# Merging the score and value visits of a banded attention kernel, with zero products in TensorE's planned gaps

## The chip, the cores and the metric

The kernel runs on one core of one Trainium2 chip. The metric is the time of one execution on the device in microseconds. The kernel before takes 534.74 us, the median of three runs (534.62 to 535.40).

## The reference

Eight batches, eight heads, 576 positions, 64 channels a head; then a gated MLP over the 4608 tokens, from 512 to 1024 and back to 512 channels. The weights arrive as 64-bit floats.

```python
# attention, B, H, S, D = 8, 8, 576, 64; stride = 32
scores = scale * np.matmul(q, k.transpose(0, 1, 3, 2))
mask_local = (rel >= 0) & (rel < stride)                       # heads 0 to 3
mask_strided = (rel >= 0) & (pos[None] % stride == pos[:, None] % stride)  # heads 4 to 7
scores = np.where(masks, scores, -1000000000.0)
scores = scores - np.max(scores, axis=-1, keepdims=True)
attn = np.exp(scores)
attn = attn / (np.sum(attn, axis=-1, keepdims=True) + 1e-09)
x = (attn @ v).transpose(0, 2, 1, 3).reshape(B, S, H * D)
# gated MLP: w_in 512 x 1024, conv_w 3 x 1024, w_out 1024 x 512
h = np.maximum(x @ w_in, 0.0)
conv_out[:, s] = sum(conv_w[k] * h[:, s + k - 1] for k in range(3))
gate = 1.0 / (1.0 + np.exp(-conv_out))
return (h * gate @ w_out).astype(np.float32)
```

## The kernel before

**Attention** works on items: item n is a pair of heads of one batch, and there are 32 (four to a batch). Both masks are banded in blocks of 32 rows once the positions of the strided heads are reordered, so an item's scores are ten blocks of 64 columns on 128 partitions, 128 x 640. TensorE writes the mask as a product (L449) and adds the scores (L458). VectorE takes the maximum (L470) and subtracts it (L471), ScalarE takes the exponent (L473), VectorE sums (L474) and inverts (L476). Then the result is divided and turned in one of two ways, chosen by `TURN`: GpSimd multiplies (L492) and VectorE transposes (L494), or VectorE makes a diagonal of the inverses (L478), TensorE multiplies by it (L486) and ScalarE copies the result (L490). The values product (L514) gives 128 x 576. It leaves PSUM as two parts, a high one by a ScalarE cast (`xh`, L549) and a low one by a VectorE subtraction (`xl`, L574). For the first four items `LOW` chooses another way for the low part: TensorE subtracts the high part in PSUM (L569) and ScalarE copies the rest (L572).

**The MLP** runs over nine groups g of 512 tokens. The first layer (L607) has eight column blocks f, each the sum over four channel blocks, the second (L667) four output blocks over eight f. Each product is made of three matmuls of 128x512, high by high, low by high, high by low; such a triple is the unit of TensorE's order. Between the layers a column block takes relu (L624), a scaling by the middle tap (L634 or L637), two multiply-adds (L643), a sigmoid (L646), the gate (L648) and a split into high and low parts (L431, L434). Ahead of all that, the weights are converted from 64-bit words (L334 to L343, eight times 128 x 1024) and split, partly with products by the unit matrix on TensorE (`wA`, L411 to L413; `wQ`, L418 and L419).

**PSUM.** A tile `psR` of 2048 columns, four banks, belongs to attention; four single banks `m` belong to the MLP and the weights. Item n's scores stand in half n % 2 of `psR`, columns 192 to 832 of the half; the values of every item stand in columns 352 to 640 of both halves. Their columns overlap, and both carry the same keys:

```python
ks = [("R", n % 2)]                # scores, maximum, subtraction
ko = [("R", 0), ("R", 1)]          # values, xh, xl
```

**What sets the order.** Nothing is emitted as it is written. Each operation is recorded by `op(engine, duration, at, function, reads, writes)` in a `Plan`. `Plan.order` simulates the engines with these durations; whenever an engine is free it takes, of what is ready, the operation with the least number `at`. The numbers are the tables at the head of the file (`FIRST_AT`, `AT`, `ATTENTION_AT`, `MM2_AT` and so on). `emit` then calls the functions in the order found, and semaphores are set by what the instructions touch. The order is therefore fixed at build time, one queue to an engine, and all DMAs go through SyncE.

In `attention(n, at)`, scores and softmax of item n are recorded and then the values of item n - 1, as two operations of TensorE, each a visit between triples of the MLP. Before the first work and around the first items TensorE runs small bf16 products of zeros (L686, L465, L523), their numbers given by `WARM`, `WARM_SCORES` and `WARM_VALUES`.

Of the kernel before, what the change touches and what calls it, by code (L numbers as in the profile page):

```python
# [10 lines left out]
F32 = _mybir.dt.float32  # L11
# [20 lines left out]
SWITCH = 0.1  # L32

EYE_AT = -5641.81
MASK_AT = [-976.49, -4840.98]
CONV_AT = -1964.94
FIRST = "q0 v3 c0 w2 q1 v1 q3 q2 w0 v0 w1 v2"
WARM = 4
WARM_SCORES = [2, 16, 0, 2]
WARM_VALUES = [0, 4, 2, 2]  # L40
FIRST_AT = [-11728.54, 2927.8, 1156.62, 10403.26, -3568.28]
CG = [-1145.22, 2936.15, 5191.78, 6866.73, -374.84, 2714.75, -185.49, -2874.38]
FIRST_CG = [5953.58, -4528.01, -140473.56, -26915.48, 1020.79, 13500.44, -7471.53, 1012.12]
AT = [-1263.9, -35606.56, -37908.55, 2094.87, 4457.14, -6773.99, -185.12, -4417.32, -12155.9, 1673.67, 15790.05, 21190.07]
FIRST_AT_OP = [-4532.44, -1425.97, -13901.61, 3673.25, -1290.91, 1763.1, -479.55, 1634.23, -15895.84, 6131.84, 16717.04, 7502.42]
GROUP_AT = [-432.81, 2274.65, -1090.97, -2015.72, 1599.72, 153.86, -492.27, -1297.65, -11802.33]
MM1_STEP = 182.77
MM2_AT = [587.25, -1866.84, 1305.83, 4267.84, 3322.73, -2070.19, -331.06, -2597.74, 7549.41]
MM2_STEP = 9285.75
ATTENTION_AT = [[684.23, -3321.47, -12257.54, -3438.78], [-4223.53, -19768.27, -12237.56, 1866.03], [1591.41, 1584.68, 22534.87, -7346.12], [-3831.37, -1063.8, 3506.54, -355.28], [-1239.26, 6530.18, 6237.55, -6386.36], [-13104.5, -763.71, -32188.48, 2649.73], [4064.36, -26150.52, -3567.23, 311.36]]  # L50
LOAD_Q = -4833.81
LOAD_V = 4648.5
W_IN_AT = [-5962.99, 2980.22, -1315.38, 6776.79]
W_OUT_AT = [-1481.2, -11386.53, 419.86, -2531.25]
SPLIT_W = "aaqaaaaq"
SPLIT_G = "vvpvvpvp"
FIRST_SPLIT_G = "vvvppvvv"
MAJOR = 0
FIRST_GATE = "vvvvvppp"
FIRST_SCALE = "vavaaaaa"  # L60
TURN = "pvvvv"
LOW = "pppp"


class Plan:
# [25 lines left out]
    def order(self, at):  # L91
# [13 lines left out]
        idle, hot = 0.0, 0.0  # L105
# [3 lines left out]
        while True:  # L109
# [32 lines left out]
            if e == "pe":  # L142
                if ops[i][5] != kind:
                    kind = ops[i][5]
                    t += SWITCH
                if t - idle > 3.4:
                    hot = t + 3.5
                if t < hot:
                    dur = min(2 * dur, dur + (hot - t) / 2)
                idle = t + dur  # L150
# [17 lines left out]
        return [i for _, i in out], begin, end  # L168

# [73 lines left out]
    def emit(self):  # L243
        order, self.begin, self.end = self.best()
        for i in order:
            self.ops[i][3]()
# [3 lines left out]
def tile_banded_attention_gated_mlp(ctx, tc, qkT, vw, w_in, conv, w_out, masks_in, picks_in, eye_in, out):  # L250
# [186 lines left out]
    def probabilities(n, at):  # L437
# [5 lines left out]
        scores_ = psS[:, 192:192 + 2 * NBLK * 64]  # L443
        ks = [("R", n % 2)]

        def scores():
            for c in range(NSEG):
                for h in range(2):
                    nc.tensor.matmul(psS[W * c:W * c + W, 192 + 320 * h:512 + 320 * h], picks[64 * h:64 * h + 64, c % 2],  # L449
                                     masks[64 * h:64 * h + 64, kind, c // 2], start=True, stop=False,  # L450
                                     tile_position=(64 * h, W * c), skip_group_check=True)
            for m in range(NBLK):
                for c in range(NSEG):
                    if SEGS[c] + m < SEGS[c + 1]:
                        s = W * (SEGS[c] + m)
                        for h in range(2):
                            o = 192 + 320 * h + 64 * m
# [3 lines left out]

        if n < NHP and WARM_SCORES[n]:
            def warm_s():
                for _ in range(WARM_SCORES[n]):
                    nc.tensor.matmul(psS[:, 832:1024], warm_[:, :P], warm_[:, :192], start=True, stop=True)  # L465
# [332 lines left out]
```

## Time and profile before

| | |
|---|---|
| median of three runs | 534.74 us (534.62 to 535.40) |
| the profiled execution's own time | 534.35 us |
| its span in the trace | 532.2 us |
| TensorE busy | 511.5 us |
| VectorE busy | 362.3 us |
| ScalarE busy | 319.7 us |
| GpSimd busy | 118.3 us |
| mean granted TensorE clock | 0.987 |

The span is the time between the first and the last instruction in the trace; the execution's own time has 2.15 us more around it. In lines of the profile a row gives line, engine, operation, output and input with their shapes, the count, and busy time or start. TensorE's matmuls are pipelined, so that one of 0.39 us starts 0.23 us after the one before it; costs on TensorE are read from start to start. r is `psR`, m one of the four banks, t and tt the probabilities before and after transposition, qk and v the inputs of an item.

### The profile page before, as it was taken

How to read it: one execution, taken by the hardware profiler on the slowest of the kernel's cores; microseconds unless marked ns; L12 is line 12 of the kernel's file. 1: busy time of each engine (PE TensorE's matmuls, PEld its weight loads, DVE VectorE, ACT ScalarE, POOL GpSimd, SP SyncE). 2: the span in 40 equal slices, each digit the busy share in tenths (PEclk: the TensorE clock that was granted, in tenths of full speed). 3: DMA queues.
4: the chain of work that ended last, by engine and by line, in shares of the span. 5: the costliest groups of instructions: out<-in, count | busy, mean ns of one | idle time of the engine just before them, and what ended most of it. 6: DMA issues, size and time to landing. Idle time of an engine off the chain costs nothing.

```text
span 532.2 us, 16633 instructions
## 1 busy us (share of the span) xinstructions
PE 511.5 (96%) x7352; PEld 410.3 (77%) x7352; DVE 362.3 (68%) x639; ACT 319.7 (60%) x492; POOL 118.3 (22%) x197
## 2 busy tenths in 40 slices
PE   4788999999999999999999999999999999999997
PEld 3555677778877887788778877887788778888897
DVE  3978789966785668757965784688658845832840
ACT  2454777856684658556737675577557755633841
POOL 0111202432222112212232222132212221320210
PEclk9797999999999999999999999999999999999999
DMA  8656412452044303521333044303430001001001
GB/s 287 245 185 229 156 69 78 126 186 76 13 137 150 90 3 130 184 72 30 118 102 137 1 124 151 113 0 123 137 127 2 32 16 66 1 13 67 0 32 48
DMA packets 17639, 51.30 MB, mean 96 GB/s; under 512 B 2208, under 2 KB 3360, under 8 KB 17568
## 3 DMA queue, kind: packets, MB, share of 16 engines
q1 hardware_dynamic: 17568, 50.25, 28.2%
q8 instruction: 57, 0.93, 0.7%
q14 instruction: 14, 0.11, 0.1%
HBM read 40.80 MB, written 9.44 MB: 94 GB/s over the span
## 4 chain that ended last, share of the span: by engine, by line
PE 93%; ACT 2%; DVE 2%; DMA 1%; issue 1%; SPq 1%; DVEq 0%; ACTq 0%
PE m L667 40%; PE m L607 37%; PE r L514 6%; PE r L458 4%; PE m L411 2%; PE r L449 1%; DMA misc<-in_dram 1%; PE r L569 1%; PE m L413 0%; PE m L412 0%; ACT xh L549 0%; PE r L486 0%; DVE t L471 0%; DVE mx L470 0%; ACT wa L334 0%
## 5 line engine op out<-in xcount | busy, mean ns | idle before, releaser
L643 DVE SCALAR_TENSOR_TENSOR misc<-misc,cw 128x512 f32<-128x512 f32 (+29 forms) x256 | 127.9, 546 | 35.9 <-ACT misc L634 35.3
L667 PE MATMUL m<-gh,woh 128*128 128x512 f32 (+2 forms) x320 | 124.2, 388 | 0.0
L667 PE MATMUL m<-gh,wol 128*128 128x512 f32 (+2 forms) x320 | 119.0, 372 | 0.0
L667 PE MATMUL m<-gl,woh 128*128 128x512 f32 (+2 forms) x320 | 119.0, 372 | 0.0
L607 PE MATMUL m<-xh,wih 128*128 128x512 f32 x288 | 113.3, 393 | 0.0
L607 PE MATMUL m<-xh,wil 128*128 128x512 f32 x288 | 112.5, 391 | 0.0
L607 PE MATMUL m<-xl,wih 128*128 128x512 f32 x288 | 112.5, 391 | 0.0
L492 POOL TENSOR_TENSOR t<-t,sm 128x640 f32<-128x640 f32 x31 | 45.3, 1462 | 116.6 <-DVE sm L476 84.0
L667 PEld LDWEIGHTS m<-gh,woh 128*128 128x128 f32 x320 | 60.1, 188 | 12.5
L624 ACT ACTIVATE misc<-m 128x512 f32<-128x512 f32 x72 | 42.9, 596 | 43.8 <-PE m L607 42.1
L667 PEld LDWEIGHTS m<-gl,woh 128*128 128x128 f32 x320 | 60.2, 188 | 11.4
L667 PEld LDWEIGHTS m<-gh,wol 128*128 128x128 f32 x320 | 60.2, 188 | 9.1
L607 PEld LDWEIGHTS m<-xh,wih 128*128 128x128 f32 x288 | 54.1, 188 | 11.8 <-issue 0.2
L607 PEld LDWEIGHTS m<-xl,wih 128*128 128x128 f32 x288 | 54.2, 188 | 11.5
L607 PEld LDWEIGHTS m<-xh,wil 128*128 128x128 f32 x288 | 54.2, 188 | 11.2
L634 ACT ACTIVATE misc<-misc,cw 128x512 f32<-128x512 f32 (+1 forms) x70 | 50.5, 724 | 11.4 <-DVE gl L434 5.3
L648 DVE TENSOR_TENSOR misc<-misc 128x512 f32<-128x512 f32 (+1 forms) x69 | 47.8, 693 | 13.2 <-ACT misc L646 12.9
L646 ACT ACTIVATE misc<-misc 128x512 f32<-128x512 f32 (+1 forms) x72 | 44.6, 627 | 15.0 <-DVE misc L643 14.3
L431 ACT CAST gh<-misc 128x512 fp32r<-128x512 f32 (+1 forms) x72 | 44.3, 620 | 13.1 <-DVE misc L648 11.3
L673 ACT COPY misc<-m 128x512 f32<-128x512 f32 (+2 forms) x40 | 21.5, 545 | 48.0 <-PE m L667 47.4
L626 POOL COPY misc<-carry 128x2 f32<-128x2 f32 x64 | 19.1, 299 | 132.6 <-DVE misc L648 93.2
L470 DVE TENSOR_REDUCE mx<-r 128x10 f32<-128x640 f32 x32 | 26.2, 820 | 30.9 <-PE r L458 30.9
(84 smaller groups left out, 584.6 us busy)
## 6 DMA issues: line engine op xcount, KB each, us to landing
qk<-in_dram SPq DMA_DIRECT2D x32, 592.0 KB, 3.9
v<-in_dram SPq DMA_DIRECT2D x32, 384.0 KB, 3.5
ws<-in_dram SPq DMA_DIRECT2D x14, 512.0 KB, 4.5
out_dram<-misc SPq DMA_DIRECT2D x28, 256.0 KB, 3.1
misc<-in_dram SPq DMA_DIRECT2D x2, 512.0 KB, 6.2
out_dram<-misc SPq DMA_DIRECT2D x4, 255.5 KB, 3.5
out_dram<-misc SPq DMA_DIRECT2D x3, 256.5 KB, 2.0
masks<-in_dram SPq DMA_DIRECT2D x2, 160.0 KB, 2.3
```

What stands on the lines that cost most here:

```text
L431: op(A, ta, at, lambda: nc.scalar.copy(hi(), src), [skey], [(key, "h")])
L470: op(V, 0.826, at + offset[0], lambda: nc.vector.tensor_reduce(out=mx, in_=p3, axis=AX.X, op=ALU.max), ks, [("mx", i)])
L492: op(G, 1.28, at + offset[5], lambda: nc.gpsimd.tensor_tensor(out=t, in0=t, in1=sm.unsqueeze(2).to_broadcast([P, 2 * NBLK, 64]), op=ALU.mu ...
L514: nc.tensor.matmul(psV[64 * h:64 * h + 64, o:o + n_], v[W * c:W * c + W, h, j], tt[W * c:W * c + W, 64 * NBLK * h + a:64 * NBLK * h + z], ...
L607: nc.tensor.matmul(ps, a[:, c, fs], x[:, c, N * x0:N * x0 + N], start=(n == 0 and m == 0), stop=(n == NC - 1 and m == 2))
L624: op(A, 0.596, at + cg[2], lambda: nc.scalar.activation(out=h[:, 2:N + 2], in_=ps, func=AF.Relu), [kp], [("h", hi)])
L634: op(A, 0.725, at + cg[3], lambda: nc.scalar.activation(out=c_[:, :n], in_=h[:, 1:n + 1], func=AF.Copy, scale=w1), kh + ["cw"], [kc] + new)
L643: op(V, 0.11 + 0.00117 * (z - a), at + cg[4] + 0.4 * k, lambda k=k, wk=wk, a=a, z=z: nc.vector.scalar_tensor_tensor(out=c_[:, a:z], in0=h[ ...
L646: op(A, 0.63, at + cg[5], lambda: nc.scalar.activation(out=c_[:, :n], in_=c_[:, :n], func=AF.Sigmoid), [kc], [kc], table=1)
L648: op(ge, 0.69 if ge == V else 1.28, at + cg[6], lambda: (nc.vector if ge == V else nc.gpsimd).tensor_tensor(out=c_[:, :n], in0=h[:, 1:n + ...
L667: nc.tensor.matmul(ps, a[:, f, ms], y[:, f, tok], start=(f == 0 and n == 0), stop=(f == NF - 1 and n == 2))
L673: op(A, 0.59 if z - a0 == N else 0.38, at + 3 * t + 3, lambda ps=ps, a0=a0, z=z: nc.scalar.copy(o[:, a0:z], ps), [("M", mi)], ko)
```

## The change

- Scores move to columns 0 to 320 and 640 to 960 of their half, one range for each head, and get a key of their own (`S`); the values keep 352 to 640 (key `O`). From item 4 on, the scores of item n + 1 and the values of item n are one operation `both_`, without triples between them. An operation that uses either waits for both.
- The bf16 warm-up products go. `emit` looks at the gap that the plan leaves on TensorE ahead of each operation and puts f32 products of zeros into it, 64 x 64, on columns 960 to 1024 of `psR` (`busy`). In the built program they are 130, in groups of 26, 61, 6, 7, 4 and 26, all ahead of the stream of the MLP.
- `TURN`: the first, second and fourth items are turned by TensorE, before only the first. `LOW`: one item's low part is made on TensorE, before all four; the other three are VectorE's.
- All tables of numbers are others, and the planner counts TensorE's clock and its changes of shape in another way. The first DMAs come in another order. `SPLIT_G`, `FIRST_SPLIT_G`, `FIRST_GATE` and `FIRST_SCALE` give some of the first group's work to another engine.

```diff
-WARM = 4
-WARM_SCORES = [2, 16, 0, 2]
-WARM_VALUES = [0, 4, 2, 2]
+COLD = 7.0
+FILL = [0.3, 0.12, 0.22]
...
-FIRST = "q0 v3 c0 w2 q1 v1 q3 q2 w0 v0 w1 v2"
+FIRST = "q0 w2 w0 v2 q1 v1 v0 q2 v3 c0 q3 w1"
...
-MM2_STEP = 9285.75
+MM2_STEP = 15743.9
...
-SPLIT_W = "aaqaaaaq"
-SPLIT_G = "vvpvvpvp"
-FIRST_SPLIT_G = "vvvppvvv"
+SPLIT_W = "aaaaaqaq"
+SPLIT_G = "vvvpvpvv"
+FIRST_SPLIT_G = "pvvppppp"
-FIRST_GATE = "vvvvvppp"
-FIRST_SCALE = "vavaaaaa"
-TURN = "pvvvv"
-LOW = "pppp"
+FIRST_GATE = "vvpvpvpp"
+FIRST_SCALE = "vaaaavva"
+TURN = "ppvpv"
+LOW = "vpvv"
...
-    def emit(self):
-        order, self.begin, self.end = self.best()
+    def emit(self, busy):
+        order, begin, end = self.best()
+        last = 0.0
         for i in order:
+            if self.ops[i][0] == "pe":
+                for _ in range(int((begin[i] - last - FILL[0]) / (FILL[2] if last < COLD else FILL[1]))):
+                    busy()
+                last = end[i]
             self.ops[i][3]()
...
-        scores_ = psS[:, 192:192 + 2 * NBLK * 64]
-        ks = [("R", n % 2)]
+        two = psR[:, 1024 * (n % 2):1024 * (n % 2) + 960].rearrange("p (x c) -> p x c", c=NBLK * 64)[:, 0:3:2]
+        ks = [("S", n % 2)]
+        bits = ["bits"] if n <= 2 * NHP else []
...
-        op(T, 0.92, at, scores, [("qk", i), ("mask", kind), "picks"], ks, table=1)
+        if join is None:
+            op(T, 0.89, at, scores, [("qk", i), ("mask", kind), "picks"], ks + bits, table=1)
+        else:
+            def both_():
+                scores()
+                join[0]()
+            op(T, 1.88, at, both_, [("qk", i), ("mask", kind), "picks"] + join[1], ks + join[2] + bits, table=1)
...
-        ko = [("R", 0), ("R", 1)]
+        ko = ["O"]
...
-        op(T, 0.94, at + offset[7], products, [("tt", i), ("v", i)], ko, table=2)
+        if n >= NHP and n + 1 < B * NHP:
+            probabilities(n + 1, later, (products, [("tt", i), ("v", i)], ko))
+        else:
+            op(T, 0.91, at + offset[7], products, [("tt", i), ("v", i)] + (["bits"] if n < NHP else []), ko, table=2)
...
-        if n < B * NHP:
+        if n <= NHP:
             probabilities(n, at)
         if late:
-            values(*late.pop())
+            values(*late.pop(), at)
...
-    warm_ = const.tile([P, 256], BF16, name="warm")
...
+    warm_ = const.tile([P, 64], F32, name="warm")
+
+    def busy(start=False):
+        nc.tensor.matmul(psR[0:64, 960:1024], warm_, warm_, start=start, stop=True, skip_group_check=True)
```

What this does to TensorE's order is seen at three places. First, a values visit in the middle of the stream before: TensorE's rows there, between two triples of the first layer (tt and v with a number are buffers, m_94 is one bank).

```order
L607 MATMUL m_94<-xh,wil 128x512
L607 MATMUL m_94<-xl,wih 128x512
L514 MATMUL r<-tt_61,v_59 64x32 x6
L514 MATMUL r<-tt_61,v_59 64x64 x26
L514 MATMUL r<-tt_61,v_59 64x32 x2
L514 MATMUL r<-tt_61,v_59 64x64 x2
L514 MATMUL r<-tt_61,v_59 64x32 x6
L607 MATMUL m_94<-xh,wih 128x512
```

The values stand alone; the scores of the next item come at another place. The same engine at a visit of the changed kernel, from the last of its mask products on:

```order
L455 LDWEIGHTS picks
L455 MATMUL r<-masks,picks 32x320
L464 MATMUL r<-qk_58 32x64 x36
L522 MATMUL r<-tt_67,v_65 64x32 x6
L522 MATMUL r<-tt_67,v_65 64x64 x26
L522 MATMUL r<-tt_67,v_65 64x32 x2
L522 MATMUL r<-tt_67,v_65 64x64 x2
L522 MATMUL r<-tt_67,v_65 64x32 x6
L673 MATMUL m_93<-gh,woh 128x512
L673 MATMUL m_93<-gh,wol 128x512
```

The values have moved behind the scores of the next item, and no triple stands between them. Second, the start: TensorE's rows before, around the transposition of the first item (diag is the diagonal of inverses, m_93 a bank that a weight block is split in).

```order
L449 LDWEIGHTS picks
L449 MATMUL r<-masks,picks 32x320
L458 MATMUL r<-qk_64 32x64 x36
L486 MATMUL r<-diag,t_60 32x32 x80
L411 MATMUL m_93<-misc,eye 128x512
L412 MATMUL m_93<-wl_101,eyer 128x512
L413 MATMUL m_93<-wih,negr 128x512
L514 MATMUL r<-tt_61,v_59 64x32 x6
```

And the changed kernel's TensorE around the same transposition, ahead of it the scores of the first item:

```order
L455 MATMUL r<-masks,picks 32x320
L464 MATMUL r<-qk_58 32x64 x36
L690 MATMUL r<-warm 64x64 x61
L494 MATMUL r<-diag,t_60 32x32 x80
L455 LDWEIGHTS picks
L455 MATMUL r<-masks,picks 32x320
```

The transposition has moved ahead of the second item's scores and stands directly behind 61 zero products; the first of these waits for VectorE's first subtraction, which reads the same tile. Third, TensorE at the last large group of zero products (m_95 and m_96 are banks of the second layer, m_93 that of the first layer's next column block):

```order
L673 MATMUL m_96<-gh,woh 128x512
L673 MATMUL m_96<-gh,wol 128x512
L673 MATMUL m_96<-gl,woh 128x512
L690 MATMUL r<-warm 64x64 x26
L613 MATMUL m_93<-xh,wih 128x512
L613 MATMUL m_93<-xh,wil 128x512
```

These 26 stand among the triples of the first MLP group, where before no product of zeros stood; they wait for a VectorE instruction that reads `psR` (a low part, L580), and the triple behind them waits for a relu on ScalarE that frees its bank.

VectorE's order at a steady merged visit shows what reads `psR` after it, in the changed kernel (mx is the maximum, t the difference, xl the low part of the values):

```order
L477 TENSOR_REDUCE mx0_62<-r_92 128x10
L580 TENSOR_TENSOR xl_76<-r_92,xh_75 128x576
L478 TENSOR_TENSOR t0_60<-r_92,mx0_62 128x10x64
L482 TENSOR_REDUCE sm0_63<-t0_60 128x10
```

The low part stands between the maximum and the subtraction. In the built program the cast that makes `xh` on ScalarE and the maximum wait for one another, although their columns differ.

More of the change, by code (lines that the diff above doesn't have):

```diff
@@ L104, in order @@
         moved = 0.0
-        idle, hot = 0.0, 0.0
         table = kind = None
@@ L168, in order, with switch @@
         return [i for _, i in out], begin, end
+    @staticmethod
+    def switch(a, b):
+        x, y = a in (1, 2, 3), b in (1, 2, 3)
+        return SWITCH[0] if x and y else SWITCH[1] if y else SWITCH[2] if x else 0.0
     def latest(self, rank):
@@ L494, in probabilities, with values @@
         op(V, 0.863, at + offset[6], lambda: nc.vector.transpose(out=tt.rearrange("p (u c) -> p u c", c=64), in_=t), [("t", i)], [("tt", i)])
-    def values(n, at):
+    def values(n, at, later):
         i, hp = slot(n), HPS[n % NHP]
@@ L518, in products @@
                         begun.add((c, h))
-        if n < NHP and WARM_VALUES[n]:
-            def warm():
-                for _ in range(WARM_VALUES[n]):
-                    nc.tensor.matmul(psV[:, 832:1024], warm_[:, :P], warm_[:, :192], start=True, stop=True)
-            op(T, 0.09 * WARM_VALUES[n], at + offset[7] - 0.1, warm, [("tt", i)], ko)
-        op(T, 0.94, at + offset[7], products, [("tt", i), ("v", i)], ko, table=2)
+        if n >= NHP and n + 1 < B * NHP:
+            probabilities(n + 1, later, (products, [("tt", i), ("v", i)], ko))
+        else:
+            op(T, 0.91, at + offset[7], products, [("tt", i), ("v", i)] + (["bits"] if n < NHP else []), ko, table=2)
         b = n // NHP
@@ L679, in mm2 @@
             op(Q, 256, at + 6, lambda: nc.sync.dma_start(out=out[ms, first:first + N + 1], in_=o[:, 0:N + 1]), ko, [])
-    warm_ = const.tile([P, 256], BF16, name="warm")
-    def warm_up():
-        nc.vector.memset(warm_, 0.0)
-        for _ in range(WARM):
-            nc.tensor.matmul(psR[:, 640:864], warm_[:, :P], warm_[:, :224], start=True, stop=True)
+    warm_ = const.tile([P, 64], F32, name="warm")
+    def busy(start=False):
+        nc.tensor.matmul(psR[0:64, 960:1024], warm_, warm_, start=start, stop=True, skip_group_check=True)
     with tc.manual_schedule():
-        op(T, 0.2 * WARM, -10, warm_up, (), [("R", 0)])
+        op(V, 0.1, -20, lambda: nc.vector.memset(warm_, 0.0), (), ["warm"])
+        op(T, 0.1, -10, lambda: busy(True), ["warm"], [])
         op(Q, 64, EYE_AT, lambda: nc.sync.dma_start(out=eye, in_=eye_in), (), ["eye"])
@@ L735, in tile_banded_attention_gated_mlp @@
                 mm2(g, m, t0 + MM2_AT[g] + MM2_STEP * m)
-        plan.emit()
+        plan.emit(busy)
 def _masks(S):
```

69 lines of the change are left out of this document (31 added, 38 removed).

## The prediction

> **What bounds the kernel now.** I read the page's totals first, then its slices, then the shares of the chain that ended last.
>
> ```profile
> span 532.2 us, 16633 instructions
> ...
> PE 511.5 (96%) x7352; PEld 410.3 (77%) x7352; DVE 362.3 (68%) x639; ACT 319.7 (60%) x492; POOL 118.3 (22%) x197
> ...
> PE   4788999999999999999999999999999999999997
> ...
> PEclk9797999999999999999999999999999999999999
> ...
> PE 93%; ACT 2%; DVE 2%; DMA 1%; issue 1%; SPq 1%; DVEq 0%; ACTq 0%
> ```
>
> TensorE is busy for 96% of the span and holds 93% of the chain. Only the first five or six slices have gaps, and two of them a reduced clock. So I cut the span where the stream becomes whole, at the visit that computes the scores of item 5; these are busy times by stretch, in the order PE, PEld, DVE, ACT, POOL, then the granted clock:
>
> ```profile
> 0.00:11.83 11.83, 4.25 (x96) 3.49 (x97) 3.50 (x13) 2.67 (x4) 0.36 (x6) 1.00 0.83 271
> 11.83:82.06 70.23, 60.70 (x1015) 44.19 (x1020) 58.88 (x79) 40.22 (x54) 10.53 (x12) 0.90 0.51 176
> 82.06:505.79 423.73, 423.73 (x6062) 340.02 (x6063) 293.75 (x541) 269.62 (x420) 105.20 (x177) 1.00 0.25 82
> ```
>
> From 82.06 to 505.79 TensorE has no idle time at full clock, so the time there is the sum of what it executes. Before 82.06 VectorE is the fuller engine for its tasks: 3.50 + 58.88 = 62.4 us busy, 19.7 idle. The kernel is therefore a start of 82 us, led by conversions and the first softmaxes, and a stream in which only TensorE's own cost counts. The units of the stream come from the end of the chain of waits (start, length, matmuls):
>
> ```profile
> 464.50 19.49 PE m L667 x84
> 483.99 21.80 PE m L607 x96
> 505.79 22.82 PE m L667 x192
> ```
>
> Three matmuls form one product in high and low parts, a triple: 21.80/32 = 0.68 us for the first layer, 19.49/28 = 0.696 for the second, 22.82/64 = 0.357 for the half-wide ones of the last group. The last matmul ends at 528.6, the span at 532.2: a tail of 3.6.
>
> **Part 1: one visit in place of two.** The timeline of TensorE around one scores visit and one values visit (start, length):
>
> ```profile
> 151.85 0.39 PE L667 MATMUL m<-gl,woh 128*128 128x512 f32 x1
> 152.17 0.33 PE L449 MATMUL r<-masks,picks 64*32 64x320 bf16 x8
> 152.31 0.95 PE L458 MATMUL r<-qk 64*32 64x64 f32 x72
> 153.19 0.50 PE L667 MATMUL m<-gh,woh 128*128 128x512 f32 x1
> 153.53 0.40 PE L667 MATMUL m<-gh,wol 128*128 128x512 f32 x1
> ...
> 155.87 0.39 PE L667 MATMUL m<-gl,woh 128*128 128x512 f32 x1
> 156.19 1.12 PE L514 MATMUL r<-tt,v 32*64 32x32 f32 x84
> 157.24 0.51 PE L667 MATMUL m<-gh,woh 128*128 128x512 f32 x1
> 157.58 0.40 PE L667 MATMUL m<-gh,wol 128*128 128x512 f32 x1
> ```
>
> The undisturbed step is 0.696/3 = 0.232. Into the scores it is 152.17 - 151.85 = 0.32, an entry of 0.09; out of them the first step is 153.53 - 153.19 = 0.34, an exit of 0.11. The whole scores visit costs 153.53 - 151.85 - 2 x 0.232 = 1.22, the values visit 157.58 - 155.87 - 0.46 = 1.25, the pair 2.47. Merging removes one exit and one entry, 0.20, and adds a junction from scores to values which this trace never shows. Bounds: a free junction saves s = 0.20; one as dear as exit and entry together saves 0. I take the middle between a free junction and an entry, 0.045, so s = 0.155.
>
> The junction changes the shape of the array's tiles from 64*32 to 32*64. [...]
>
> Visits with both parts start at item 4's values; 27 are made, 26 lie behind the start. The gain is 26 x 0.155 = 4.0 us, bounds 0 and 5.2.
>
> **Part 2: the work left behind the start.** In the new order the stream becomes whole behind the last group of 26 zero products. Counted from the two orders, before has from 82.06: 258 x 0.68 + 256 x 0.696 + 22.8 + 27 x 1.22 + 28 x 1.25 + 3.6 = 447.9, so 530.0 against the 532.2 found: 2.2 us of small steps that I carry over. After has 264 x 0.68 + 254 x 0.696 + 22.8 + 26 x 2.47 + 1.25 + 3.6 = 448.2, less 4.0 and plus 2.2: 446.4 behind the fillers. The start is level if that last group ends at 81.8.
>
> **Part 3: when the start ends.** That group's last wait is on VectorE, and the relu that frees the next bank follows the gate of column block 1, VectorE's too. So I count VectorE. Groups of its instructions in 0 to 82.06 (busy, mean ns, idle before):
>
> ```profile
> L335 DVE TENSOR_SCALAR wa<-wa 128x1024 f32<-128x1024 f32 x8 | 5.5, 688 | 5.1 <-ACT wa L334 5.1
> ...
> L474 DVE TENSOR_REDUCE sm<-t 128x10 f32<-128x650 f32 x5 | 4.1, 821 | 0.0
> ...
> L470 DVE TENSOR_REDUCE mx<-r 128x10 f32<-128x640 f32 x5 | 4.0, 809 | 3.4 <-PE r L458 3.4
> L494 DVE STREAM_TRANSPOSE tt<-t 128x640 f32<-128x640 f32 x4 | 3.3, 837 | 1.1 <-POOL t L492 1.1
> ...
> L434 DVE TENSOR_TENSOR gl<-misc,gh 128x512 fp32r<-128x512 f32 x2 | 1.4, 686 | 0.0
> ...
> L476 DVE RECIPROCAL sm<-sm 128x10 f32<-128x10 f32 x5 | 1.0, 207 | 0.0
> ...
> L478 DVE TENSOR_TENSOR diag<-small,sm 128x320 f32<-128x320 f32 x1 | 0.5, 480 | 0.0
> ```
>
> Up to that gate the new order adds one softmax (0.81 + 0.81 + 0.82 + 0.21), the low parts of three items and half of a fourth (about 3.1 at the 0.76 shown below) and two diagonals (1.0). It drops two transposes (1.7), two low parts of gates (1.4) and two smaller scalings (1.2). Together +2.4: 64.8 us busy. Idle: before had 8.3 up to 11.83 and 11.4 behind. The early part holds loads and the first exponent, and I take 9.3, a little longer as scores start behind 26 fillers. Of the later 11.4, the waits for GpSimd (1.1) shrink and conversions wait less for loads that come in another order; walking through the order's waits with these durations I get 7, with 0 and 11.4 as ends. The gate then ends at 64.8 + 9.3 + 7 = 81.1.
>
> The fillers cost something here. One conversion block of three matmuls costs, by two starts that surround one:
>
> ```profile
> 30.84 1.06 PE L411 MATMUL m<-ws,eye 128*128 128x512 f32 x2
> ...
> 32.22 0.51 PE L523 MATMUL r<-warm 128*128 128x192 bf16 x4
> ```
>
> 1.38, of which the f32 one is 1.38 - 0.46 = 0.92 for 512 columns: 64 columns would be 0.115, and I take 0.12 a filler at full clock. 26 of them take 3.1 and wait for a low part that VectorE finishes about 1.5 ahead of the gate, near 79.6. They end at 82.7, while the relu ends at 81.8: about 0.9 lost. I take 82.8, 1.0 behind level. Ends: without later idle 75, with before's 86.7.
>
> The other fillers (26, 61, 6, 7, 4) fill known waits, and cost nothing while these cover them. The group of 61 stands ahead of the first transposition and waits for VectorE's first subtraction near 9.9; at 0.12 it ends at 17.2, when the diagonal is about ready.
>
> **Sum.** 82.8 + 446.4 = 529.2, with the 2.15 that the before execution has around its span 531.3, against its 534.35. The runs' median is 0.39 above that execution, so 531.7.
>
> **Rival: the first fillers run at half clock (slower).** The clock by stretch (PE busy, clock):
>
> ```profile
> 27.20:30.70 3.50, 2.33 (x84) 1.00 0.18 25
> ...
> 40.90:44.30 3.40, 2.01 (x92) 0.99 1.00 376
> 44.30:47.70 3.40, 3.02 (x83) 0.50 0.23 73
> 47.70:51.10 3.40, 3.40 (x7) 0.50 0.66 182
> ```
>
> After a stretch 59% busy the clock fell to 0.50 for two stretches; after one 67% busy it stayed. A filler is 64 x 64 in size, a short instruction on a quarter of the array, and whether it counts as activity no row says. For the rival: the wait for the subtraction itself leaves TensorE idle. Against: fillers remove the gaps. Half clock throughout makes 61 x 0.24 = 14.6, the first transposition starts at 24.5 instead of 17.2 and the whole start goes 7.3 later: 539.0. Half clock at the head alone gives 1.8, 533.5. It decides once that transposition starts later than VectorE's next free time, about 17.3 to 20.
>
> **Rival: softmax longer than the spacing.** Scores and values are now written together, so VectorE's reading of the scores and ScalarE's evacuation of the values become ready together. In the built program these are put one behind the other, although their columns differ: the reduction waits for the cast, or the reverse, often with the low part between. Durations:
>
> ```profile
> 162.85 0.79 DVE L471 TENSOR_TENSOR t<-r,mx 128x640 f32<-128x640 f32 x1
> ...
> 163.67 0.74 ACT L473 ACTIVATE t<-t 128x640 f32<-128x640 f32 x1 [1.92 <-DVE t L471]
> ...
> 165.39 0.64 ACT L549 CAST xh<-r 128x576 fp32r<-128x576 f32 x1 [0.97 <-PE r L514]
> ...
> 166.06 0.76 DVE L574 TENSOR_TENSOR xl<-r,xh 128x576 fp32r<-128x576 f32 x1 [0.78 <-ACT xh L549]
> ...
> 167.67 1.25 POOL L492 TENSOR_TENSOR t<-t,sm 128x640 f32<-128x640 f32 x1
> ```
>
> From a visit to its transposed result: 0.64 + 0.82 + 0.76 + 0.79 + 0.74 + 0.82 + 0.21 + 1.25 + 0.84 = 6.9, some 7.4 with handovers, 1.4 of it new. The next merged visit, which needs it, comes after mostly 12 to 14 triples (8.3 to 9.7 us) and four times after 10 or 11 (6.9 to 7.7, plus the scores' own 1.0 ahead of the values). It fits, barely at the four. Behind a late cast stand relu and sigmoid on ScalarE, then the banks of the first layer. If it missed by 0.5 at half of the visits, 12 x 0.5 = 6 us: 537.7. [...]
>
> **Rival: a dear junction.** With s = 0 the saving is gone: 535.7. **Rival: all goes well.** With s = 0.20 and VectorE's idle at 5 instead of 7, fillers end near 81: 528.7.
>
> **How the numbers follow.** The forecast has 0.48 (530 to 533.5), all-goes-well 0.17, the dear junction 0.13, half clock 0.13, softmax 0.09. About 0.2%, 533.7 to 535.8, can't be told from no change here. Faster: the first two less a little for a start nearer its late end, 0.63. Same: most of the dear junction and the mild half clock, 0.14. Slower: 0.23. The range 527.8 to 538.0 leaves out the full half clock and a start more than 2 us early.
>
> **What would show it.** In the new trace: merged visits of 2.3 us; a last filler group ending near 82.8; the clock near 1.0 from the first fillers on, the first transposition near 17; no idle time of TensorE ahead of values matmuls from 90 us on. A transposition at 20 or later, gaps ahead of merged visits, or a visit of 2.47 make it wrong.

## The result and the profile after

| | before | changed |
|---|---|---|
| median of four runs | 535.07 us (534.62 to 537.76) | 552.19 us (548.97 to 553.30) |
| ratio, 95% interval | | 1.0299 (1.0244 to 1.0355) |
| profiled execution, span | 534.35, 532.2 | 548.97, 547.2 |

The change makes the kernel 3% slower; 531.7 was forecast, with 538.0 as the upper end. Of the 18.0 us by which the profiled span exceeds the sum's 529.2, the start brings 15.3 and the rest 2.7, as the stretches below show. The page of the changed kernel, the same five lines:

```profile
span 547.2 us, 17672 instructions
...
PE 521.2 (95%) x7876; PEld 424.2 (78%) x7876; DVE 365.9 (67%) x646; ACT 319.1 (58%) x492; POOL 111.6 (20%) x192
...
PE   7679698999999989999999999999999999999997
...
PEclk9999699999999999999999999999999999999999
...
PE 86%; DVE 7%; issue 3%; ACT 2%; DMA 1%; SPq 0%; POOL 0%; ACTq 0%; DVEq 0%; POOLq 0%
```

TensorE is still the bound, but the gaps at the start now reach into the seventh slice, and "issue", time in which the engine waited for nothing that the profile shows, has grown from 1% to 3% of the chain. The stretches, cut where the last group of zero products ends:

```profile
0.00:98.12 98.12, 78.66 (x1782) 60.79 (x1782) 65.29 (x98) 46.80 (x62) 8.87 (x18) 0.93 0.49 170
98.12:521.00 422.88, 419.58 (x5904) 340.70 (x5903) 293.46 (x540) 264.40 (x414) 99.83 (x173) 1.00 0.23 79
```

The start ends at 98.1, not at 82.8. VectorE's work in it is 65.3 (64.8 was forecast up to the gate, which ends at 96.2; up to there it is 64.6); its idle time is 32.8 and not 16.3. Behind it 547.2 - 98.1 = 449.1 remain, where 450.4 less the saving of the merges was to be expected: nearly nothing was saved. A merged visit by itself does what it should (TensorE's timeline, start and length):

```profile
126.22 0.39 PE L673 MATMUL m<-gl,woh 128*128 128x512 f32 x1
126.54 0.33 PE L455 MATMUL r<-masks,picks 64*32 64x320 bf16 x8
126.69 0.94 PE L464 MATMUL r<-qk 64*32 64x64 f32 x72
127.56 1.11 PE L522 MATMUL r<-tt,v 32*64 32x32 f32 x84
128.61 0.50 PE L673 MATMUL m<-gh,woh 128*128 128x512 f32 x1
128.94 0.40 PE L673 MATMUL m<-gh,wol 128*128 128x512 f32 x1
```

From 126.22 to 128.94, less two steps of 0.232, it costs 2.26 where the pair cost 2.47: s = 0.21. The junction is free, 0.87 from the first scores to the first values against 0.88 for scores alone. But another visit reads:

```profile
190.55 0.33 PE L455 MATMUL r<-masks,picks 64*32 64x320 bf16 x8
190.70 0.95 PE L464 MATMUL r<-qk 64*32 64x64 f32 x72
191.57 1.03 PE L522 MATMUL r<-tt,v 32*64 32x32 f32 x75
194.13 0.32 PE L522 MATMUL r<-tt,v 32*64 32x32 f32 x9 [1.52 <-issue]
```

TensorE stops in the middle of one product's list of matmuls, 1.74 from start to start, and no semaphore is waited for. All waits of this kind, from the list of TensorE's waits in the changed kernel (total, times, longest):

```profile
PE r L522 <- issue: 6.0, 4, 2.6
PE r L464 <- issue: 2.1, 2, 1.9
...
PE m L613 <- issue: 1.4, 1, 1.4
...
PE r L494 <- issue: 0.3, 1, 0.3
```

Counting TensorE's records in the trace (weight loads, matmuls, semaphore instructions) ahead of each gives the same place every time (at is the start of the last matmul before the wait):

```
at us    in      start to start   records ahead   modulo 256
 18.70   turning      0.49              705           193
 20.56   scores       2.09              961           193
 34.82   values       1.84             1472           192
 53.90   values       2.77             2497           193
 59.88   scores       0.53             2753           193
192.38   values       1.74             6848           192
399.66   values       0.60            13249           193
419.91   layer 1      1.87            13760           192
```

Where it is 192, the weight load had gone ahead and the matmul behind it waits. So counted, 193 records modulo 256 have started at every wait. The page has two DMA queues of kind instruction; the larger reads:

```profile
q8 instruction: 61, 1.00, 0.7%
```

61 packets of 16,384 bytes; before there were 57. TensorE has 15,788 records here, 61.7 times 256. In all 16 traces of this study, from 9,777 to 15,820 records and from 38 to 62 packets, the number of packets is that of the records plus 64, divided by 256 and rounded down. In the trace the packet that belongs to the wait at 192.38 begins at 191.66 and takes 1.17; TensorE goes on 1.30 after its end. In all eight cases it goes on 1.2 to 1.5 after the end of a packet on q8. So the theory, inferred from these counts and times, was: **TensorE's code arrives in pieces of 256 instructions, and it waits when it uses one up sooner than the next arrives.** A merged visit is 328 instructions in 2.1 us (in the trace each f32 product of the attention is two weight loads and two matmuls: the 36 of a scores visit stand as x72); a scores visit of before was 160, then a triple of 6 in 0.69. The rivals were the guard on the banks, the fillers, the clock, and merging itself. By the guard I mean the waits between readers of `psR` whose columns differ; in the changed page the cast waits 37.8 us for the maximum:

```profile
L555 ACT CAST xh<-r 128x576 fp32r<-128x576 f32 (+13 forms) x56 | 23.4, 433 | 61.0 <-DVE mx L477 37.8
```

For all kernels below I cut the profiled executions at equal work; the medians are those of all runs. Work is the sum of the MLP's matmuls at 0.2275 and 0.232 (0.119 half wide) and of scores and values at 1.03 and 1.05 (0.55 and 0.58 in all_bf16); lost time is the time less the work done. "Start" is the loss when 40 us of work are done, "stream" what is lost behind. "Code" is the part of the stream's loss in waits at records 192 to 194 of 256 that end 1.2 to 1.6 behind a packet. The stream's loss includes the entries and exits of the visits, about 0.2 each. The start differs by some 2 us between executions of the same order: 69.1, 71.9, and 71.6 with 1.0 of added products in it (changed, after_apart, fill_plus8).

| kernel | median | start | stream | code |
|---|---|---|---|---|
| before | 534.5 to 535.7 | 53.8 | 10.4 | 0.0 |
| changed | 552.2 | 69.1 | 10.5 | 3.9 |
| no_fill | 553.2 | 72.2 | 13.3 | 4.9 |
| fill_plus8 | 563.4 | 71.6 | 20.4 | 11.3 |
| after_apart | 549.1 | 71.9 | 9.1 | 0.7 |
| turn_bf16 | 552.6 | 61.5 | 22.1 | 10.1 |
| all_bf16 | 513.0 | 61.5 | 13.6 | 0.0 |
| one_turn | 547.2 | 58.8 | 18.4 | 7.7 |
| old_keys | 559.9 | 67.6 | 21.0 | 6.7 |
| start_before | 542.4 | 62.2 | 10.7 | 3.7 |
| merge_good | 550.3 | 56.4 | 22.7 | 1.3 |
| merge_bad | 558.5 | 55.6 | 33.3 | 12.3 |
| merge_guard | 551.5 | 57.2 | 23.7 | 1.8 |
| merge_spaced | 554.1 | 56.7 | 32.2 | 8.4 |
| merge_apart | 546.6 | 56.5 | 20.6 | 0.0 |
| merge_later | 544.0 | 57.4 | 17.9 | 0.0 |

### The profile page after: what moved, and what is told of

It reads as the page before. It is cut to its first block, busy times and chain, and to the rows that moved or that the text cites. A ratio compares the mean times of both kernels' runs of the same rounds, so it can differ in the third digit from the quotient of the medians.

```text
span 547.2 us, 17672 instructions
## 1 busy us (share of the span) xinstructions
PE 521.2 (95%) x7876; PEld 424.2 (78%) x7876; DVE 365.9 (67%) x646; ACT 319.1 (58%) x492; POOL 111.6 (20%) x192
## 4 chain that ended last, share of the span: by engine, by line
PE 86%; DVE 7%; issue 3%; ACT 2%; DMA 1%; SPq 0%; POOL 0%; ACTq 0%; DVEq 0%; POOLq 0%
PE m L613 35%; PE m L673 35%; PE r L522 6%; PE r L464 4%; PE r L455 1%; PE m L416 1%; DMA misc<-in_dram 1%; DVE misc L649 1%; DVE mx L477 1%; PE r L690 1%; PE r L494 1%; DVE xl L580 1%; ACT xh L555 1%; DVE sm L482 1%; DVE t L478 1%
## 5 line engine op out<-in xcount | busy, mean ns | idle before, releaser
L649 DVE SCALAR_TENSOR_TENSOR misc<-misc,cw 128x512 f32<-128x512 f32 (+28 forms) x256 | 124.8, 538 | 27.4 <-ACT misc L640 26.8
L673 PE MATMUL m<-gh,woh 128*128 128x512 f32 (+2 forms) x320 | 121.0, 378 | 0.0
L500 POOL TENSOR_TENSOR t<-t,sm 128x640 f32<-128x640 f32 x29 | 39.8, 1371 | 128.7 <-DVE sm L484 114.1
L477 DVE TENSOR_REDUCE mx<-r 128x10 f32<-128x640 f32 x32 | 26.4, 824 | 50.8 <-PE r L522 31.2
L555 ACT CAST xh<-r 128x576 fp32r<-128x576 f32 (+13 forms) x56 | 23.4, 433 | 61.0 <-DVE mx L477 37.8
L630 ACT ACTIVATE misc<-m 128x512 f32<-128x512 f32 x72 | 42.4, 595 | 22.2 <-PE m L613 21.4
L640 ACT ACTIVATE misc<-misc,cw 128x512 f32<-128x512 f32 (+1 forms) x69 | 49.1, 725 | 8.0 <-POOL misc L632 2.9
L632 POOL COPY misc<-carry 128x2 f32<-128x2 f32 x64 | 22.6, 355 | 140.9 <-DVE misc L654 94.1
L654 DVE TENSOR_TENSOR misc<-misc 128x512 f32<-128x512 f32 (+1 forms) x68 | 46.1, 704 | 4.8 <-ACT misc L652 4.7
```

The costliest lines, as they stand in the source:

```text
L477: op(V, 0.826, at + offset[0], lambda: nc.vector.tensor_reduce(out=mx.rearrange("p (h u) -> p h u", h=2), in_=p4, axis=AX.X, op=ALU.max), ...
L500: op(G, 1.28, at + offset[5], lambda: nc.gpsimd.tensor_tensor(out=t, in0=t, in1=sm.unsqueeze(2).to_broadcast([P, 2 * NBLK, 64]), op=ALU.mu ...
L555: op(A, 0.162 + 0.00083 * (z - a), at + offset[8], lambda hi=hi, src=src: nc.scalar.copy(hi, src), ko, [("xh", hp, x) for x in halves])
L630: op(A, 0.596, at + cg[2], lambda: nc.scalar.activation(out=h[:, 2:N + 2], in_=ps, func=AF.Relu), [kp], [("h", hi)])
L640: op(A, 0.725, at + cg[3], lambda: nc.scalar.activation(out=c_[:, :n], in_=h[:, 1:n + 1], func=AF.Copy, scale=w1), kh + ["cw"], [kc] + new)
L649: op(V, 0.11 + 0.00117 * (z - a), at + cg[4] + 0.4 * k, lambda k=k, wk=wk, a=a, z=z: nc.vector.scalar_tensor_tensor(out=c_[:, a:z], in0=h[ ...
```

## The experiments

**1. No fillers.** `emit` inserts nothing; the order is the same.

```diff
-                for _ in range(int((begin[i] - last - FILL[0]) / (FILL[2] if last < COLD else FILL[1]))):
-                    busy()
```

> The changed kernel without the 129 zero products that fill planned gaps. Theory 1, code supply: in the trace of the changed kernel seven waits of TensorE that no semaphore explains stand all at the same place of its instruction stream, 192 or 193 records behind a multiple of 256, and each ends about 1.3 us after a 16 KB instruction transfer on queue q8; three of them (2.1, 1.8 and 2.8 us) stand in the start, where fillers, transposition, scores and values follow one another. The fillers are 516 of these instructions; without them the burst around the first transposition is shorter, that first wait (2.1) goes, and the kernel takes 545 to 551. The others stay, since transposition, values and scores still adjoin. Theory 2, clock: the fillers keep the clock at 1.0 in the start; without them it falls to 0.5 and the kernel takes 555 or more. Theory 3, fillers as waits: each group waits for VectorE's reading of the same tile and then delays it, in sum 5 to 8 us: 544 to 547, with the 1.8 and 2.8 us waits still there.

Measured 553.22 (ratio to before 1.0332, 1.0279 to 1.0385): no gain, no loss against 552.19 (548.97 to 553.30; here 551.50 to 554.84). All three theories missed their numbers; waits at 192 or 193 of 256 came at 20.1, 32.1, 35.8, 54.5 and 88.0 us (2.3, 2.1, 2.2, 3.4, 1.5), at other matmuls, with up to 516 records fewer ahead. The fillers are neither the loss nor a help.

**2. Eight more fillers ahead of the stream.**

```diff
-                for _ in range(int((begin[i] - last - FILL[0]) / (FILL[2] if last < COLD else FILL[1]))):
+                gap = int((begin[i] - last - FILL[0]) / (FILL[2] if last < COLD else FILL[1]))
+                for _ in range(gap + 8 if gap > 20 and last > 40 else gap):
```

> The changed kernel with 34 in place of 26 zero products in the last group, ahead of the MLP's stream: 32 more instructions, so that every later piece of 256 begins 32 instructions earlier in the work. Theory 1, code supply: a merged visit of 328 instructions waits where a piece begins some 43 to 85 instructions after its head. Behind the last group these are five visits now (about 5 us); shifted by 32 it would be seven to eight others, about 10.8 us in sum, so the kernel takes 5.7 + 1.0 (eight products at 0.12) more: 557 to 560, with waits again only at 192 or 193 of 256. Theory 2, only the added work counts: 0.8 to 1.0 more, 553, with the waits at the same visits as before.

Measured 563.36, 11 more than the changed kernel where 6.7 (557 to 560) was expected and 0.8 to 1.0 by the rival. Code waits in the stream went from 3.9 in three to 11.3 in seven, as forecast in size and place; some 3 us more were lost in two stretches of 3.4 at half clock behind them, and the start was 2.5 later in this execution, 1.0 of it the eight products.

**3. and 4. Merging alone, with two counts of zero products at the very beginning.** The kernel before with the new columns and `both_`, without the rest of the change; the twins differ in one number.

```diff
+        for _ in range(13):      # merge_bad: 42
+            nc.tensor.matmul(psR[:, 640:704], warm_[:, :P], warm_[:, :64], start=True, stop=True)
```

> The kernel before with one part of the change alone: scores in columns of their own and merged visits from item 4 on; its start, tables, turning and low parts are kept, its bf16 zero products stand in columns 960 to 1024 (three narrow ones for each), and 13 more of them at the very beginning. Theory 1, code supply: the start ends as before, at 82; 26 merged visits save 0.25 each (the junction showed no cost in the changed kernel: 2.07 to 2.08 us a visit), 6.5; with this number of instructions ahead, one visit stands badly to the pieces of 256 (the 14th of the merged ones), 1.5: 530. Theory 2, the loss of the changed kernel lies in merging itself (softmax longer than the spacing of merged visits): gaps ahead of merged visits at other places than 193 of 256, 535 or more. Theory 3, phase doesn't matter: the same as with 42 products at the beginning.

> As the kernel with 13 more zero products at the beginning, but with 42 of them, all in the time in which TensorE waits for the first loads: 58 instructions more ahead of everything, and the same work. Theory 1, code supply: ten of the merged visits now hold a piece's beginning 40 to 90 instructions after their head, eight of them with 0.5 to 1.7 us of wait, 11.9 in sum: 540, some 10 more than its twin. Theory 2 and 3: no difference to the twin beyond 0.5.

Measured 550.28 and 558.45. The 8.2 between them come from 29 zero products placed where TensorE waits for loads (4.5 in merge_good, 3.8 in merge_bad): their starts lose the same (56.4 and 55.6), the code waits of the stream 1.3 and 12.3 (1.5 and 11.9 expected). TensorE's waits behind the start, first merge_good:

```profile
PE r L521 <- DVE tt L501: 5.9, 3, 2.5
PE m L617 <- ACT xh L559: 2.3, 3, 1.4
PE m L677 <- ACT misc L634: 2.2, 2, 1.4
PE m L677 <- issue: 1.0, 1, 1.0
```

then merge_bad:

```profile
PE r L521 <- issue: 7.8, 7, 1.7
PE r L521 <- DVE tt L501: 4.5, 3, 2.5
...
PE m L677 <- ACT xh L559: 1.7, 1, 1.7
...
PE m L677 <- issue: 0.9, 1, 0.9
```

The 1.7 put down to a high part stands at record 194 of 256, 1.3 behind a packet, and is a code wait too. So between these two the phase decides about the code waits. But the two are 20 and 18 above their forecasts, and merge_good shows what else: values that wait for their transposed probabilities, triples that wait for high parts and for relu. Theory 2 holds here, beside theory 1.

In these kernels the offset at which a piece begins within a visit tells whether it waits. From the 135 merged visits of the changed kernel and of these four, with the wait at the piece's end, 256 records on:

```
records from the visit's head to the piece's beginning     wait (start to start)
up to 35                                                   none in 16 of 17, 1.3 in one
37 to 43                                                   0.2 to 0.9
44 to 79                                                   1.1 to 2.0 in all 20 visits
81 to 93                                                   by code at most 0.2 over a step
94 and more                                                none by code
```

**5. One item turned by TensorE.** `TURN = "pvvvv"`, no fillers.

> The changed kernel without fillers (552.2 with, 553.2 without) and with one item turned by TensorE as before, not three; the planner orders the rest anew. Theory 1, bursts of code in the start: in the kernel without fillers TensorE still waits at 192 or 193 of 256 five times before 99 us, 11.5 us in sum, each time inside a row of transposition, values and scores (642 and 648 instructions without a triple between). Two transpositions of 320 instructions less leave one long row; the stream begins at 88 to 94 in place of 98 and the kernel takes 543 to 549, with the stalls of the stream that its new phase gives (some 7). Theory 2, the guard on the banks: the planner believes that scores and values don't touch, the built program puts the readers of both behind one another and behind the next visit; that is left as it is, so the start ends at 96 to 99 and the time is 551 to 555.

Measured 547.25, in theory 1's range. The start loses 58.8 against 72.2, and 2.8 of code waits against 11.4. The planner made another order, so this says that the turned items go with the loss, not how.

**6. The same three items, half the code.** No fillers, and the same order as kernel 1.

```diff
-    ta[W * c:W * c + W, u, W * x:W * x + W], diag[W * c:W * c + W, u],
+    ta.bitcast(BF16)[W * c:W * c + W, u, 2 * W * x + 1:2 * W * x + 2 * W:2], diag.bitcast(BF16)[W * c:W * c + W, u, 1:2 * W:2],
```

> The changed kernel without fillers and in the same order; the three transpositions on TensorE read the upper halves of the same f32 words as bf16, so that each is 160 instructions and not 320 (the probabilities of these three items are cut to bf16). Theory 1, code supply in the start: the rows of 642, 649 and 648 instructions become 481, 489 and 488; the four waits inside them (2.3, 2.1, 2.2 and 3.4 us in the kernel without fillers) fall to one of about 1 to 2 in each row, and the stream of the MLP begins 5 to 9 us earlier. In the stream its phase is a worse one (10.9 against 6.7 of stalls), so the whole takes 547 to 551 against 553.2. Theory 2, the guard on the banks: the transposition saves only its own 0.7 us each; the stream begins 2 us earlier at most, and the whole takes 555 or more.

The start: the same triple of the first layer, behind the same wait for relu, in the kernel without fillers and in this one:

```profile
98.47 0.79 PE L611 MATMUL m<-xh,wih 128*128 128x512 f32 x1 [3.38 <-ACT misc L628]
```

```profile
89.00 0.67 PE L611 MATMUL m<-xh,wih 128*128 128x512 f32 x1 [3.39 <-ACT misc L628]
```

9.5 earlier, of which the shorter matmuls are some 2. Theory 2's bound for the start (2) falls. Code waits in the start went from 11.4 to 5.2. VectorE shows what they hold up: its work up to this triple is the same (64.3 and 64.6), but its waits ahead of instructions that read `psR` (maximum, subtraction, low part) fall from 26.4 to 16.7. The longest group of them, without fillers and then with half the code:

```profile
DVE xl L578 <- ACT xh L553: 11.8, 2, 6.8
```

```profile
DVE xl L578 <- ACT xh L553: 4.7, 2, 2.8
```

The whole is 552.62, above theory 1's 547 to 551: the stream's phase was as bad as foreseen (10.1), and some 5 us more, by my estimate, were lost at half clock behind such waits (mean clock 0.98 from 89.0 us to 520, 0.99 from 98.5 to 520 in the kernel without fillers).

**7. The planner's keys of before.** `ks = [("R", n % 2)]`, `ko = [("R", 0), ("R", 1)]` again, no fillers.

> The changed kernel without fillers, and in the planner's records the keys of before: values write what both halves' scores write, so that the planner itself lets a values visit wait for the softmax's readers and the next scores for the evacuation. Columns, merging and the built program's own guards stay. Theory 2, the guard: the order of the start now fits the waits that the program has; the start ends 5 to 10 us earlier, 88 to 93, and the time is 544 to 549 (its stream has phase stalls of about 9 against 6 of the kernel without fillers). Theory 1, bursts: two of three rows in the start lose their scores (648 becomes 490), so less than 3 us: 551 to 555.

Measured 559.94: both theories' numbers missed. With the guard in the plan the start loses 67.6 against 72.2, but weight blocks then wait 6.7 for VectorE, and the eighth triple of the first group begins 9 us later (82.3 against 73.1). The other tables weren't made for these keys, so this neither shows nor refutes the guard.

**8. The start's tables of before in the changed kernel,** no fillers, 19 zero products at the beginning.

> The changed kernel without fillers, its start ordered with the tables and choices of before (first loads, offsets of the first items, conversions, first group, one item turned by TensorE, four low parts by TensorE), the later groups with its own tables, and 19 zero products of 64 columns at the very beginning, 76 instructions, for a phase with few stalls (two visits, 3.9 in sum). Both theories: the loss of the start goes, the stream begins at 82 to 86, the merged visits save 6.5, stalls cost 4 and up to 2 more for the clock behind them: 533 to 539. If the loss comes from the later groups (softmax behind the shared banks), 545 or more.

Measured 542.37, 3 above the range. The start loses 62.2, where before lost 53.8 and the changed kernel 69.1, and this without a code wait in it: it isn't the start of before, since the planner's costs differ. A weight block waits 6.3 for a conversion, and 37.5 us of the start run at half clock, 13.6 in before. The stream loses 10.7 with 3.7 of code, as expected.

**9. One engine at a time on a bank, in the plan.** merge_good with this condition in `order` and 5 zero products:

```diff
+                    for b in range(4):
+                        if ops[i][7] >> b & 1 and by[b] != e:
+                            w = max(w, held[b])
```

> The kernel before with own columns and merged visits (as in the pair of kernels with 13 and 42 products), the planner now told that two engines may not use one bank of the attention tile at the same time, so that its order spaces merged visits by 11 to 15 triples mostly; 5 zero products at the beginning for a phase with one bad visit (1.9). The kernel with 13 took 550.3: its trace has 1.5 of code waits, but 4.0 to 5.9 us of values waiting for their transposed probabilities, 5 us of triples waiting for high parts of values or for relu, and some 5 us at half clock behind such waits. Theory 2, the guard and the spacing: with the order aware of it these go, and the kernel takes 530 to 536. If merging in itself costs (values late whatever the spacing), above 543.

Measured 551.50, above 543: the rival's side. Code waits in the stream are 1.8, but values still wait 4.3 for probabilities, triples 3.2 for high parts.

**10. and 11. More room ahead of each merged visit** (the later groups' visits are also due 12000 earlier in `ATTENTION_AT`), and the badly standing ones taken apart:

```diff
-            return t + 0.1
+            return t + (0.1 + 2.0 if self.ops[i][1] == 1.88 and a == "dve" else 0.1)
...
+            if i in soon:        # merge_apart only: scores three triples ahead
+                soon[i]()
```

> The kernel before, merged and with the planner's guard on banks as in the last kernel of this kind (551.5), but with 2 us of slack ahead of each merged visit in the plan and the visits of later groups due earlier: spacing 12 triples or more in the stream. With 5 zero products at the beginning its phase has seven visits that wait, 9.2 in sum, and the clock behind them. Theory 1: start as before, 26 x 0.2 saved, 9.2 and 3 to 6 for the clock lost: 539 to 545, no values waiting for their probabilities. Theory 2, merging costs in another way: values or triples still wait for softmax or high parts, above 546.

> The same kernel, with the scores of the eight visits that stand badly emitted three triples ahead of their values (items 7, 9, 12, 15, 18, 27, 29 and 30). Theory 1: the code waits go: start as before (1 to 2 late for the zero products), 18 visits at 0.2 saved, some 0.5 of remaining waits: 531 to 534, faster than the kernel before. If the waits follow the visits: as its twin.

Measured 554.06 and 546.64. Taking eight visits apart took all 8.4 of code waits out of the stream and some 4 of half clock; 7.4 in the medians. Neither reached its number: some 7 us of waits by semaphore are left in both streams, 5.4 of them first-layer triples that wait for high and low parts. The last visit of a batch is tied to the next scores, which may be why its values come late; this was not tested.

**12. The same in the changed kernel:** four of its visits taken apart, the rest unchanged.

> The changed kernel with its fillers; at four of its 27 merged visits, those with a piece's beginning 43 to 82 instructions behind their head (scores of items 13, 26, 28 and 29), the scores are emitted three triples ahead of the values, all else in the same order. Theory 1, code supply: the waits at 192, 399 and 420 us (1.7, 0.6, 1.9, with 2 us at half clock behind the last) go, four visits cost 0.2 more: 3 to 5 us less, 547 to 549. If these waits have another cause that follows the visits: no gain, 552 to 553.

Measured 549.12, 3.1 less, at the edge of the range; but the runs overlap (548.60 to 550.34 against 548.97 to 553.30), so the gain is not clear of noise. What the trace shows is that the waits at 192, 399 and 420 are gone. The stream loses 9.1 and not 10.5, with 0.7 of code waits and one new wait of 1.0 for a relu; the profiled execution of the changed kernel had no half clock behind its waits that could be saved: its clock was 1.00 from 66.2 us to the end of the span.

**13. All attention products in half the code.** As kernel 6, scores and values too.

> The changed kernel without fillers, in the same order; now scores, values and the three transpositions all read the upper halves of their f32 words as bf16, so a merged visit is 172 instructions in place of 328 (the attention is computed from cut numbers). Each visit also does half the work: some 0.5 us less for each of 32 scores and 32 values, about 32 us. Theory 1, code supply: no wait at a multiple of 256 is left to speak of; the start loses its 11 us of them, the stream its waits and the half clock behind them (about 8): 553 - 32 - 19, 498 to 506, and the stream begins at 80 to 87. Theory 2, the rest of the start's delay is the order itself and the guard on the banks: only the saved work of some ten visits goes from the start, which ends at 91 to 94; in all 508 to 516.

Measured 513.04, in theory 2's range. It doesn't decide: two waits of 2.2 and 3.2 at 192 and 193 remained in the start, where transposition, values and scores still adjoin, and in the stream TensorE now waits 6.2, mostly triples for low parts of gates and for relu, as its visits had become shorter (0.55 and 0.58 in place of 1.03 and 1.05). No code wait is left in the stream. The triple of experiment 6 starts at 83.8, in theory 1's 80 to 87 and not in theory 2's 91 to 94; but the start loses the same 61.5 as in kernel 6, with as much code wait (5.4 and 5.2), so what moved the triple from 89.0 is saved work.

**14. Merging on the start of before with the later groups' numbers of the change,** three visits apart, 2 zero products.

> The kernel before with own columns and merged visits, its start and planner kept, the numbers for the later groups (gates, offsets, groups, second layer, attention, low parts of gates) taken from the changed kernel; 2 zero products at the beginning, and the scores of the three visits that stand badly (items 15, 17 and 18) three triples ahead of their values. Theory 1: with the start of before, visits spaced for merging and no code waits, 23 visits save 0.2: 530 to 533, faster than before. If merging needs more than that (values later, high parts late for the first layer even in this order): 536 to 545.

Measured 544.04 (1.0181, 1.0154 to 1.0209): 1.8% longer than before, in the range for merging that needs more. No code wait in its stream, 8.2 us of waits for relu, high parts and probabilities. No kernel of the study with the reference's precision beats the one before.

## Why the prediction was wrong, point by point

- **What bounds the kernel**: right. TensorE in the stream, VectorE's chain in the start.
- **Part 1**: the term 26 x 0.155 was too small: the junction from 64*32 to 32*64 showed no cost (0.87 from the first scores to the first values, 0.88 for scores alone), where the entry from 128*128 cost 0.09 and the exit to it 0.11. That makes 0.21 a visit and 5.5 in all. But the sum left out the code waits: 3.9 of the 5.5 went back in three visits of 328 instructions, and kernel 12's trace has 0.7 of them left.
- **Part 2**: right as a count of work. 448.2 + 2.2 - 5.5 + 3.9 = 448.8, measured 449.1.
- **Part 3 failed, and with it the forecast.** VectorE's work up to the gate was right (64.6; the low parts entered as 3.1 are 2.7 by the sum's own 3.5 x 0.76, but the fourth comes in two pieces and the trace has 3.0), and so was its early idle time, 9.4 up to 11.83 where 9.3 was taken. The step that failed is "walking through the order's waits with these durations I get 7": from there to the gate VectorE was idle for 22.2. 98.1 lies beyond the 86.7 that I had called the end, for I bounded the wait by the idle time of the old order, while the new one puts 642 to 648 instructions of transposition, values and scores in a row. Ahead of instructions that read `psR` VectorE waited 3.4 in the start before, all of it ahead of the maximum:

```profile
DVE mx L470 <- PE r L458: 3.4, 2, 2.3
```

In the changed start it is 21.4, and the longest of it:

```profile
DVE xl L580 <- ACT xh L555: 8.6, 2, 6.2
DVE mx L477 <- PE r L464: 3.7, 1, 3.7
...
DVE mx L477 <- PE r L522: 3.1, 1, 3.1
DVE mx L477 <- ACT tt L498: 3.0, 1, 3.0
```

The 6.2 end behind the values visit with the 2.77 code wait and the scores visit with the 0.53. These are 3.3; the rest is a chain through `psR`, in which ScalarE's copy of the transposed item waits 5.84 for that values visit, the scores' mask products 0.84 for the copy, the cast `xh` 2.25 for the scores, and the low part the 6.2 for `xh`. Half the code in the same order takes 9.5 off, some 2 of it shorter matmuls (kernel 6), so I put code supply at about half of the 15.3, an estimate from these numbers. What stays open is the rest: in kernels 6 and 13 the start still loses 7.7 more than before, with 5 of code waits in it, and how much of that is the order and how much the shared banks was not separated.
- **"26 of them take 3.1"**: the last fillers took 3.17, as forecast; fillers as such changed nothing (kernel 1).
- **Rival of half clock in the first fillers**: no. The clock was 1.00 in the first 20 us, and the first transposition began at 17.9. The trace has the fillers as 128*64, where the MLP's matmuls stand as 128*128: half of that and not a quarter. Nor is the clock the reason for the late start: before and changed both had 13.6 us at half clock in it, with means of 0.92 and 0.93.
- **Rival of softmax longer than the spacing**: not in the changed kernel, whose stream has no wait but code's. It did come in the kernels that merge with the tables of before (5.9 in kernel 3).
- **Missing**: code supply was no rival at all, though "issue" stood in the chain with 1% (TensorE's only wait of that kind before is one of 0.3), and the groups of matmuls that the order prints were there to be counted. So were the 57 packets on q8, for 14,746 records of TensorE. In the changed trace, with 61 packets of 16,384 bytes, the eight waits took 0.5 to 2.8 us each from start to start.

## What to carry to other kernels

Count the instructions of TensorE's small products, not only their time: here visits of 328 in 2.1 us stood still for 0.2 to 2.0 us, in the changed kernel with no semaphore to wait for, where a piece of 256 began 37 to 79 records behind their head, and a seam that saved 0.2 was followed by a wait of 1.9 (419.91). Which visits waited went with the number of instructions ahead: 29 zero products more at the very beginning took the stream's code waits from 1.3 to 12.3 (merge_good, merge_bad), eight more in the last group from 3.9 to 11.3 (fill_plus8). So compare kernels with the count shifted before crediting an order. And where two operations are tied, look at what the earlier one fed.

## What the hardware showed that was not expected

- In all 16 traces q8 moved one packet of 16 KB for 256 of TensorE's records (61 for 15,788 in the changed kernel). From one piece's first record to the next one's, waits included, 3.2 to 4.0 us passed in four of the changed kernel's long waits (20.56, 34.82, 53.90, 192.38). Inside a visit 256 records last 1.5, and 16 of the 17 pieces that began at most 35 records behind a visit's head were passed in that time without a wait. How far ahead the code comes was not measured.
- The clock fell behind some waits and not behind others: after 13 of the 34 waits of 1.4 us and more in the streams of all kernels a stretch at half clock begins within 1 us. Behind the 1.94 wait at 455.48 in merge_bad eight steps of 0.42 to 0.52 follow in place of 0.232, some 1.9 us more, so that this visit cost nearly twice its wait. What decides whether it happens was not found.
